# Last full block evicted and stored in halves, and a newly made order for the opening, in a tuned attention and gated feed-forward kernel

## The chip, the cores and the metric

The kernel runs on one core of one Trainium2 chip. The metric is the device time of one execution in microseconds (us); lower is better.

Names used throughout: TensorE (PE in the profile), VectorE (DVE), ScalarE (ACT), GpSimd (POOL), SyncE (SP, which here only issues transfers). PSUM is the memory that TensorE writes; it has banks. A **filler** is a matmul of a zero tile whose result nobody needs.

## The reference, cut to what matters

```python
B, N, m, C = (4, 12416, 32, 128)        # x: 4 x 12416 x 128; inducing: 32 x 128

def mab(q, kv):
    s = scale * (q @ kv.transpose(0, 2, 1))
    a = np.exp(s - s.max(-1, keepdims=True))
    a /= a.sum(-1, keepdims=True) + 1e-09
    return a @ kv
h = mab(I, x)            # 32 inducing rows look at all tokens of a batch
y = mab(x, h)            # all tokens look at those 32 rows
# then, for all 49664 tokens: out = (sigmoid(y @ w_gate) * (y @ w_val)) @ w_out,  d_ff = 1536
```

What matters: `h` of batch 0 needs *all* tokens of that batch. Until they have landed and been summed, nothing of the feed-forward part can start. That is the opening (some 28 us of 699). The later batches' sums run beside the feed-forward work of the batch before.

## The kernel before: the parts that the change touches

The program fixes the order of every engine by a list of names. These are the openings of the lists before (`xt` transposes of the input, `s1t` scores, `hv` sums of a tile into the accumulator, `hbase` two fp32 matmuls that fold the sums of tiles 0 to 4 together, `fill10.1` ten fillers, `s2t` the next scores, `fo` folds of the weights with `h`, `G` the first gate matmuls). A name like `hv5.8` is tile 5, slices from 8 on; the lists are cut after the opening.

```python
"PE": zero xt0.0 xt0.8 indT s1t0.0 xt1.0 hv0.0 s1t0.8 xt1.8 hv0.8 xt2.0 s1t1.0 s1t1.8 xt2.8 hv1.0 hv1.8 xt3.0 s1t2.0
      xt3.8 s1t3.0 s1t2.8 hv2.0 hv3.0 fill10.1 xt4.0 xt4.8 s1t3.8 hv2.8 s1t4.0 xt5.0 s1t4.8 xt5.8 hv3.8 hv4.0 hv4.8
      xt5.13 s1t5.8 s1t5.0 hbase s1t5.13 hv5.8 hv5.0 hv5.13 s2t0 fo0.1 s2t2 fo0.0 sb0.2 ... G0.0.3 ...
"POOL": cx0.0 cx1.0 cx2.0 cx3.0 cx4.0 cx5.0 cx5.8 wo wg.0 wv.0 wg.1 wv.1 ...      # cx: casts of x; wg, wv: of the weights
```

The accumulator `ACC` is one bank of PSUM, 512 fp32 columns. The sums, the values and the fillers have columns of their own in it:

```python
hsum, hval = ACC[:, 288:320], ACC[:, 256:288]

def h_base():            # sums of tiles 0 to 4: copy out, diagonal, two fp32 matmuls back in
    hev = dve(129, fin, "hev", lambda o: DVE.tensor_copy(out=hacc[0][:, 0 : P + 1], in_=ACC[:, 0 : P + 1]))
    sbc = dve(32, [hev], "hb0", lambda o: DVE.tensor_scalar_mul(out=ssb[0][:], in0=I4[:], scalar1=hacc[0][:, P : P + 1]))

    def em(o):
        PE.matmul(hval, lhsT=hacc[0][:, 0:P], rhs=I4[:], start=False, stop=False, skip_group_check=True)
        PE.matmul(hsum, lhsT=ones[:], rhs=ssb[0][:], start=False, stop=False, skip_group_check=True)
    fin[:] = [op("PE", 0.48, [hev, sbc], "hbase", em)]

def h_first():           # h of batch 0: VectorE reads the sums and the values
    r = dve(256, fin, "hr0", lambda o: DVE.reciprocal(out=hden[0][:], in_=hsum))
    hTd[0] = dve(32, [r], "hc0", lambda o: DVE.tensor_tensor(out=hT[0][:], in0=hval, in1=hden[0][:], op=ALU.mult))

def fill(o, n):
    for _ in range(n):
        PE.matmul(ACC[:, 320:512], lhsT=ident[:], rhs=zeros[:], start=False, stop=False, skip_group_check=True)
```

The end of a block of 512 tokens, which the change splits for the last full block:

```python
e = act(nt * P, ws + os.old, f"E{b}.{u}", lambda o: ACT.activation(
    out=os.t[:, 0:nt, :], in_=(psl(w) if alone else ACC)[:, 0 : nt * P], func=AF.Copy, scale=0.5), ...)
st = op("SP", 0.6, [e], f"st{b}.{u}", lambda o: SP.dma_start(ov[b][:, 4 * u : 4 * u + nt, :], os.t[:, 0:nt, :]), tail=8.0)
```

The softmax here doesn't subtract the row's maximum and nothing guards it: scores larger than these inputs give would overflow.

## Time and profile before

| | before |
|---|---|
| time, first three runs | 698.72 us median (698.71 to 699.49) |
| span of the profiled execution | 697.18 us |
| ScalarE busy in the middle 659.7 us | 658.7 us: the bound |
| last input cast on VectorE starts (**L**) | 20.16 us |
| reciprocal `hden` starts | 24.07 us, L + 3.91 |
| first gate tanh on ScalarE starts (**T**; the kernel takes the sigmoid by way of tanh) | 27.67 us, L + 7.51 |
| last big eviction starts (**E**) | 693.31 us, T + 665.64 |
| from E to the end | 3.87 us |

I use the marks L, T and E. The sum of the four stretches is the span: 20.16 + 7.51 + 665.64 + 3.87 = 697.18. The stretch up to L is set in the main by how the input lands and differs by 0.6 us from one execution to the next (19.82 to 20.39 in the profiles below), so it is taken out of each comparison by giving the reciprocal and T from L on.

These lines are from the timeline of the kernel before, in its opening. The columns are start, duration (us), engine, source line, operation, output and inputs with their shapes, and in brackets how long the engine had been idle and what it had waited for.

```profile
20.16 0.29 DVE L635 CAST x<-ua 128x256 f16<-128x256 f32 x1 [0.35 <-DMA ua<-in_x_dram]
21.47 1.03 POOL L635 CAST wg<-tga 128x1024 f16<-128x1024 f32 x1 [0.36 <-DMA tga<-in_moe_w_gate_dram]
21.95 0.58 DVE L635 TENSOR_SCALAR ssb<-I,hacc 128x32 f32<-128x32 f32 x1
24.07 0.36 DVE L635 RECIPROCAL hden<-acc 128x32 f32<-128x32 f32 x1 [1.21 <-PE acc L635]
25.49 0.39 PE L635 MATMUL g<-wv,hT 128*32 128x512 f16 x2
27.67 1.94 ACT L635 ACTIVATE tga<-g 128x1024 f16<-128x1024 f32 x2
```

The first line is L, the last is T. The bracket of the reciprocal: VectorE was idle for 1.21 us and waited for TensorE's writes to `acc`. The fold of the big weight tile (`g<-wv,hT`) starts 1.42 us after the reciprocal, and the first tanh 2.18 us after that fold.

### The profile page before, as it was taken

Reading aid. Unit: us, or ns where it says so; the run is one execution under the profiler, and the core shown is the slowest. Engines: PE = TensorE matmul, PEld = TensorE weight load, DVE = VectorE, ACT = ScalarE, POOL = GpSimd, SP = SyncE. Lnnn points to the kernel's source line nnn. Section 1 sums busy time; section 2 is a strip of 40 time slices with the busy share of each in tenths; the row PEclk is TensorE's granted clock in tenths of the full one; section 3 lists DMA queues with packets and bytes.
Section 4 is the critical chain, followed back from the end, with each engine's and each line's share of the span. In section 5 each row is a group of like instructions: output and inputs, shape, how many; then the busy total and the mean of one; then the engine's idle time right before and its main releaser. Section 6 shows DMA issues by size and latency. Waiting matters only on the chain.

```text
span 697.2 us, 20697 instructions
## 1 busy us (share of the span) xinstructions
PE 672.5 (96%) x8325; PEld 384.6 (55%) x8325; DVE 667.4 (96%) x1130; ACT 675.3 (97%) x867; POOL 435.8 (63%) x498
## 2 busy tenths in 40 slices
PE   7899999999999999999999999999999999999997
PEld 5545555555555555555555555555555555555555
DVE  4799999999999999999999999999999999999997
ACT  4899999999999999999999999999999999999995
POOL 4446756855739657766485575775674675667664
PEclk9999999999999999999999999999999999999999
DMA  9859796693655646746556559422333222242211
GB/s 352 190 127 184 162 176 157 134 184 85 146 129 135 133 109 156 149 117 140 107 123 155 122 106 140 141 71 87 88 113 109 56 85 99 63 131 89 83 48 50
DMA packets 121874, 87.72 MB, mean 126 GB/s; under 512 B 80913, under 2 KB 105009, under 8 KB 121777
## 3 DMA queue, kind: packets, MB, share of 16 engines
q1 hardware_dynamic: 117584, 76.44, 43.1%
q0 software_dynamic: 4144, 9.93, 9.2%
q8 instruction: 65, 1.06, 0.6%
q14 instruction: 33, 0.26, 0.1%
q10 hardware_dynamic: 48, 0.02, 0.0%
HBM read 39.99 MB, written 38.01 MB: 112 GB/s over the span
## 4 chain that ended last, share of the span: by engine, by line
PE 51%; ACT 26%; DVE 12%; issue 5%; DMA 3%; POOL 2%; SPq 0%; ACTq 0%; DVEq 0%; POOLq 0%
PE acc L635 26%; ACT tga L635 20%; PE v L635 17%; DVE ua L635 12%; PE g L635 8%; ACT vs L635 3%; ACT os L635 3%; DMA ua<-in_x_dram 2%; DMA xT<-in_x_dram 1%; DMA out_dram<-os 1%; POOL sm L635 0%; SPq L635 0%; POOL ua L635 0%; POOL pt L635 0%; ACT e L635 0%
## 5 line engine op out<-in xcount | busy, mean ns | idle before, releaser
L635 DVE SCALAR_TENSOR_TENSOR ua<-tga,v 128x512 f16<-128x512 f16 x1041 | 641.4, 682 | 10.6 <-PE v L635 3.0
L635 ACT ACTIVATE tga<-g 128x1024 f16<-128x1024 f32 x576 | 569.0, 1142 | 0.6 <-PE g L635 0.4
L635 PE MATMUL acc<-wo,ua 128*128 128x128 f16 x4608 | 358.8, 220 | 3.2 <-ACT os L635 0.2
L635 PEld LDWEIGHTS <-ua 128*128 128x128 f16 x4608 | 262.4, 98 | 169.2 <-issue 160.4
L635 PE MATMUL v<-a2r,hw 32*128 32x512 f16 x1200 | 322.3, 374 | 8.6 <-DVE ua L635 4.3
L635 POOL TENSOR_TENSOR pt<-tga,vs 128x512 f32<-128x512 f16 x111 | 129.1, 1163 | 171.4 <-ACT vs L635 73.6
L635 PE MATMUL g<-a2r,hw 32*128 32x512 f16 (+1 forms) x1200 | 225.7, 376 | 3.5 <-ACT tga L635 1.9
L635 PEld LDWEIGHTS <-hw 32*128 32x128 f16 x2400 | 88.7, 91 | 110.1 <-issue 44.0
L635 POOL TENSOR_TENSOR ua<-pt,vs 128x512 f16<-128x512 f32 x111 | 140.9, 1269 | 9.9 <-issue 1.2
L635 ACT COPY vs<-v 128x512 f32<-128x512 f32 x111 | 77.6, 701 | 0.2 <-PE v L635 0.2
L635 ACT ACTIVATE os<-acc 128x512 f32<-128x512 f32 (+1 forms) x99 | 68.9, 696 | 2.5 <-PE acc L635 2.4
L635 POOL TENSOR_TENSOR sm<-sm,minus 128x16 f32<-128x16 f32 (+1 forms) x21 | 63.9, 3043 | 1.6
L635 POOL TENSOR_TENSOR a2n<-e2t,sm 128x128 f16<-128x128 f16 x96 | 37.2, 482 | 1.3 <-DVE sm L635 0.4
L635 POOL DMA_DIRECT2D x<-in_x_dram x18 | 11.2, 621 | 41.5 <-ACT tga L635 40.1
L635 POOL TENSOR_TENSOR tree<-tree 128x64 f32<-128x64 f32 (+4 forms) x69 | 23.7, 343 | 5.4
L635 POOL TENSOR_TENSOR tree<-e2t 128x256 f32<-128x256 f16 (+1 forms) x23 | 15.8, 688 | 8.3 <-DMA e2t<-e 8.3
L635 ACT ACTIVATE e<-g 128x512 f16<-128x512 f32 (+1 forms) x23 | 17.0, 737 | 0.1
L635 DVE COPY xT<-g 128x1024 f16<-128x1024 f16 (+1 forms) x12 | 8.0, 666 | 8.5 <-PE g L635 8.5
L635 ACT ACTIVATE eT<-g 128x512 f16<-128x512 f32 (+1 forms) x18 | 13.0, 721 | 0.0
L635 PE MATMUL g<-ident,x 128*128 128x128 f16 x97 | 7.6, 220 | 2.7 <-ACT x L635 1.3
L635 PE MATMUL g<-xT,hT 128*32 128x512 f16 (+1 forms) x108 | 9.4, 363 | 0.0
L635 DVE SCALAR_TENSOR_TENSOR ut<-tgt,v 128x512 f16<-128x512 f16 (+1 forms) x16 | 8.7, 550 | 0.3 <-PE v L635 0.2
(83 smaller groups left out, 153.7 us busy)
## 6 DMA issues: line engine op xcount, KB each, us to landing
out_dram<-os SPq DMA_DIRECT2D x96, 256.0 KB, 2.5
a2r<-dr SPq DMA_DIRECT2D x23, 512.0 KB, 4.6
dr<-a2p SPq DMA_DIRECT2D x19, 512.0 KB, 3.5
x<-in_x_dram POOLq DMA_DIRECT2D x15, 512.0 KB, 5.6
xT<-in_x_dram SPq DMA_DIRECT2D x6, 512.0 KB, 7.4
dr<-a2p SPq DMA_DIRECT2D x4, 640.0 KB, 3.3
x<-in_x_dram POOLq DMA_DIRECT2D x3, 544.0 KB, 7.8
ua<-in_x_dram SPq DMA_DIRECT2D x3, 512.0 KB, 11.5
```

The source lines that it names most:

```text
L635: ins = fn(*a, **k)
```

## The change

Intent, as far as the edit shows it. (1) **Ending:** the last full block's 512-column eviction is done in two of 256 columns, each with a store of half the size, the first from SyncE's queue and the second from ScalarE's, so that the first half leaves earlier. (2) **Opening:** the model from which the order lists were made gets the measured landing of the input (410 instead of 421 thousand bytes per us, and 1.25 us more for the second half of tile 4), the measured length of `ssb` and of a transfer's issue on GpSimd. The lists of the opening are then made anew. The constants are only used to make the order; the code that runs changes by the order alone.

The diff, cut to its core (ScalarE's list of the opening, cut here, is reordered in the same way; the rest of the lists only renumbers the fillers):

```diff
 "PE":
-        zero xt0.0 xt0.8 indT s1t0.0 xt1.0 hv0.0 s1t0.8 xt1.8 hv0.8 xt2.0 s1t1.0 s1t1.8 xt2.8 hv1.0 hv1.8 xt3.0 s1t2.0
-        xt3.8 s1t3.0 s1t2.8 hv2.0 hv3.0 fill10.1 xt4.0 xt4.8 s1t3.8 hv2.8 s1t4.0 xt5.0 s1t4.8 xt5.8 hv3.8 hv4.0 hv4.8
-        xt5.13 s1t5.8 s1t5.0 hbase s1t5.13 hv5.8 hv5.0 hv5.13 s2t0 fo0.1 s2t2 fo0.0 sb0.2 ...
+        zero xt0.0 xt0.8 indT s1t0.8 xt1.8 xt1.0 s1t0.0 xt2.0 s1t1.0 hv0.8 hv0.0 s1t1.8 xt2.8 s1t2.0 hv1.0 xt3.0 xt3.8
+        hv2.0 s1t2.8 s1t3.0 xt4.0 hv2.8 s1t3.8 hv3.0 hv1.8 s1t4.0 fill8.1 xt4.8 hv3.8 xt5.0 xt5.8 s1t4.8 hv4.0 xt5.13
+        s1t5.0 s1t5.8 hv4.8 s1t5.13 hv5.0 hv5.8 hv5.13 hbase fill10.2 s2t0 fo0.1 s2t2 fo0.0 sb0.2 ...
 "ACT": ... (casts and exponentials of the opening reordered)
+        T3.24.0 E3.22 E3.24 E3.23 Eh3.23 sth3.23
 "DVE":
-        ind16 xc0.0 indTc xc0.8 xc1.0 xc1.8 ... xc4.8 cx5.13 xc5.0 hev hb0 xc5.13 hr0 hc0 ...
+        xc0.0 ind16 xc0.8 indTc xc1.8 xc1.0 ... xc4.8 cx5.13 xc5.0 xc5.13 hev hb0 hr0 hc0 ...
 "POOL":
-        ... cx5.8 wo wg.0 wv.0 wg.1 wv.1 ld1.0 ...
+        ... cx5.8 wo wg.0 wg.1 wv.1 wv.0 ld1.0 ...
 def load(dst, src, nbytes, name):
-        landed[0] += nbytes / 421e3
+        landed[0] += nbytes / 410e3 + (1.25 if name == "lx4.8" else 0)
...
-        e = act(nt * P, ws + os.old, f"E{b}.{u}", ...)
+        for k in range(2 if (b, u) == (B - 1, NB - 1) else 1):
+            lo, hi = (2 * k, 2 * k + 2) if (b, u) == (B - 1, NB - 1) else (0, nt)
+            x = "h" * k
+            e = act((hi - lo) * P, ws + os.old, f"E{x}{b}.{u}", ...  os.t[:, lo:hi, :] <- [:, lo * P : hi * P] ...)
+            q, n = (ACT, "ACT") if k else (SP, "SP")
+            st = op(n, 0.6, [e], f"st{x}{b}.{u}", lambda o, lo=lo, hi=hi, q=q: q.dma_start(
+                ov[b][:, 4 * u + lo : 4 * u + hi, :], os.t[:, lo:hi, :]), tail=8.0)
...
-        st = op("SP", 0.6, [e], f"st{b}.{u}", lambda o: SP.dma_start(ov[b][:, 4 * u : 4 * u + nt, :], os.t[:, 0:nt, :]), ...)
```

On VectorE, `hev` and `hb0` (the copy `hacc` and the diagonal `ssb`) move behind the copy of the last transposes (`xc5.13`); on TensorE, `hbase` moves behind all the sums of tile 5; and `fill10.2`, ten fillers, stands between `hbase` and the rest.

## The prediction

> **What bounds the kernel now.** I read the busy table of three stretches first, then the groups, then the chain of waits of the opening, then the timeline around its ends. The table has, after the stretch and its length, the busy time of TensorE, its weight loads, VectorE, ScalarE and GpSimd, then clock, DMA share and GB/s.
>
> ```profile
> 0.00:27.60 27.60, 22.26 (x390) 15.23 (x394) 13.55 (x39) 14.82 (x30) 13.03 (x27) 1.00 0.91 305
> 27.60:687.30 659.70, 644.35 (x7867) 365.18 (x7866) 648.41 (x1083) 658.72 (x835) 420.63 (x470) 1.00 0.52 119
> 687.30:697.20 9.90, 5.93 (x76) 4.22 (x74) 5.46 (x10) 1.76 (x4) 2.12 (x2) 0.90 0.17 61
> ```
>
> In the middle ScalarE is busy 658.72 of 659.70 us: it is the bound, with 0.98 us of idle. The group line agrees:
>
> ```profile
> L635 ACT ACTIVATE tga<-g 128x1024 f16<-128x1024 f32 x576 | 569.0, 1142 | 0.6 <-PE g L635 0.4
> ```
>
> So the time is: start of the first gate tanh (27.67 us) + a rigid middle + an ending. The change's order lists differ only before the first gate and after the last, so a shift of the first tanh moves the end by the same amount. The opening ends with this chain (start, duration, what; us):
>
> ```profile
> 8.43 11.04 DMA ua<-in_x_dram
> ...
> 20.92 0.60 PE acc L635 x24
> 21.52 0.02 issue
> 21.54 0.30 DVE hacc L635
> ...
> 21.95 0.60 DVE ssb L635
> 22.55 0.04 issue
> 22.59 0.41 PE acc L635 x2
> 23.00 0.18 PE v L635 x4
> 23.19 0.86 PE acc L635 x34
> 24.05 0.02 issue
> 24.07 0.37 DVE hden L635
> ...
> 24.46 0.20 DVE hT L635
> ```
>
> The reader is to see that the input lands until about 20.1, and that four more microseconds pass until the reciprocal (hden) starts at 24.07: the sums of tiles 0 to 4 (acc x24), their copy (hacc), the diagonal (ssb), two fp32 matmuls (acc x2, called hbase here), then the sums of tile 5 (acc x34). From hT to the first tanh it is 27.67 - 24.46 = 3.21 us. The two cheap-looking things that matter below are the ten filler matmuls, which write the unused columns of acc, and the ending:
>
> ```profile
> 16.24 1.00 PE L635 MATMUL acc<-zeros,ident 128*128 128x192 f16 x10
> 17.07 0.50 PE L635 MATMUL g<-ident,x 128*128 128x128 f16 x6
> 693.31 0.60 ACT L635 ACTIVATE os<-acc 128x512 f32<-128x512 f32 x1 [2.42 <-PE acc L635]
> out_dram<-os SPq DMA_DIRECT2D x96, 256.0 KB, 2.5
> out_dram<-os SPq DMA_DIRECT2D x4, 64.0 KB, 1.9
> ```
>
> Ten fillers hold TensorE 17.07 - 16.24 = 0.83 us. After the last eviction (ends 693.91) a 256 KB store and the closing waits take until 697.2.
>
> **What the Trainium skill says.** (1) "PSUM — Partial Sum Buffer", section "PSUM bank collisions raise a hardware error": two engines may not touch one bank in one quadrant at once, whatever the columns, and the compiler puts a wait between them. The trace before has no filler just ahead of a read of acc, so it does not show the cost; the built program of the changed kernel does show such a wait (below). (2) "DMA: Bandwidth & Descriptors", "Anatomy of one DMA": about 2.0 us fixed plus bytes/436e9. That page's fit is for GpSimd's queue; it gives 2.6 us for 256 KB and 2.15 for 64 KB, and the trace has 2.5 and 1.9 on SyncE's queue: near enough. (3) Same page, "Issuing engines are not separate DMA queues": a second issuing engine saves only issue time; the issue is 0.33 us here. (4) "ScalarE: Activation LUTs", "What ACT_TABLE_LOAD costs": 186 ns + 0.833 ns a column, and neighbours overlap by 93 ns. For 512 columns 0.61; the trace has 0.60.
>
> **The change part by part: the ending.** One 512-column eviction becomes two of 256: estimated from the skill's formula 0.40 each, the second ending 0.40 + 0.40 - 0.09 = 0.71 after the start instead of 0.60. So the second half's store is issued about 0.1 later than the whole one was. Each store is 128 KB: between the trace's 1.9 (64 KB) and 2.5 (256 KB), interpolated by bytes 2.1, so 0.4 shorter; the first half's bytes are mostly out before the second's begin. Sum: +0.1 - 0.4 = **-0.3 us**.
>
> **The opening.** The order of the loads is not changed, so I expect the same landings. I walk the new order with the durations of the trace before. The transpose of the last slices waits, old and new, for the copy of tile 5's first half, which stands behind the last cast on VectorE and ends at 20.38 + 0.68 = 21.06. Old: transpose at 21.42, because 24 sum matmuls stood in front; new: 21.14. ScalarE's copy of the middle slices starts at about 20.6 instead of 21.02. So the new order is **ahead by 0.3 to 0.4 us** here. Then:
> - Exponentials of tile 4's half: ScalarE 21.2 to 21.6; their sums 21.8 to 22.1; copy hacc 22.1 to 22.4; ssb 22.5 to 23.1 (0.29 and 0.58 as before). Old: hacc at 21.54. The new order puts hacc **0.6 later**.
> - The program's waits show that tile 5's sums now wait for hacc (same bank): 22.5. The 34 matmuls take 0.86: to about 23.3.
> - hbase now comes last, after them: two fp32 matmuls, about 0.3 each (their weight loads are 0.30 for two): to about 24.0. In the old order these lay in the wait for the last copy and cost almost nothing at the end.
> - Then ten fillers, new here: 0.83, to about 24.8. In the built program the reciprocal's wait counts up to **the last of these fillers**; before it counted up to the last sum of tile 5. With the old 0.2 us from the last issue to the reciprocal (23.86 to 24.07): the reciprocal at about **25.0 instead of 24.07, +0.9 us**.
> - Weights: GpSimd casts now the two small tiles before the big value tile. The small ones land at about 23.4 and 24.1 (issue at 13.55 and 14.84 plus 9.8 and 9.3), so the big one ends at 24.1 + 0.6 + 1.0 = 25.75; its fold stood at 25.49. With the shift above the fold would be at 26.4: hidden.
> From hT on, the order is the old one: the first tanh at 27.67 + 0.9 = 28.6.
>
> Sum: 698.72 + 0.9 - 0.3 = **699.3 us**.
>
> **Rivals.** (a) The wait on the fillers costs nothing, or they run while the reciprocal's inputs are still pending: then the reciprocal is at about 24.15 to 24.2, +0.1. Now the weight cast binds: fold at 25.8 instead of 25.49, +0.3 at the first tanh. Total 698.72 + 0.3 - 0.3 = 698.7. Against it: the wait is in the program. (b) The plan of the change holds: last tile 0.3 earlier, carried through, and the ending's 0.3: 698.1. For it: the PE stalls between 15.6 and 21 are real. Against it: hbase and the copy moved behind the last sums, and the landing itself does not move. (c) The second store is slower than thought (both share the same 16 engines, and ScalarE's queue was last used at 0.72 us): ending 0, total 699.6. (d) The early part falls behind: the first projection of scores moves from 7.99 to about 8.5, and the casts of ScalarE up to 12.7 are delayed by up to 0.7. Landings are 1.25 us apart and each tile needs 0.7 of VectorE and about 1.1 of TensorE, so I expect it caught up by tile 4, which lands 1.2 late (17.37).
>
> **Range and chances.** The opening's sum has an error of about 0.4 (six estimated steps of 0.1 to 0.2), the ending's 0.15, and the three runs before spread over 0.8. Rival (a) is inside the range, (b) outside. 8 in 10: 698.6 to 700.0. 2% is 14 us, some ten times anything here: within 2% 0.98.
>
> **What would show it.** In the changed profile: reciprocal hden at 24.8 to 25.3, directly after ten fillers; hacc at 22.1; first transpose of the last four slices near 21.15; first gate tanh at 28.3 to 28.8; two 256-column evictions of 0.37 to 0.40; from the end of the last sum (693.29 before) to the end of the span 3.6 instead of 3.9 us; middle ScalarE idle still about 1 us. I would be wrong if hden starts before the fillers end, if the first tanh is not later, or if the middle takes the shift up.

## The result, and the profile after

The changed kernel is correct. It took 699.43 us median of 4 runs (699.15 to 699.53); the kernel before, in the same rounds, 699.06 (698.71 to 699.49). The ratio of the two is 1.0004 with a 95% interval of 0.9987 to 1.0022: the same. (A ratio is the mean time of one kernel's fast runs over that of the other's of the same rounds, so it is not quite the ratio of the medians.)

The busy table of three stretches of the changed kernel, with the columns as in the prediction:

```profile
0.00:28.30 28.30, 22.88 (x394) 16.59 (x394) 12.87 (x39) 14.60 (x30) 13.10 (x27) 0.94 0.88 296
28.30:687.90 659.60, 644.16 (x7866) 365.49 (x7864) 648.04 (x1083) 658.57 (x835) 420.34 (x470) 1.00 0.53 119
687.90:697.80 9.90, 6.12 (x79) 4.33 (x76) 5.65 (x10) 2.03 (x5) 2.34 (x2) 0.95 0.18 61
```

The middle is as before: ScalarE busy for 658.57 of 659.60 us. The first tanh comes 0.86 us later (28.53 against 27.67). The opening's chain of waits (start, duration, what):

```profile
21.26 0.38 PE g L636 x4
...
22.24 0.30 DVE hacc L636
...
22.59 2.31 PE acc L636 x48
...
24.93 0.37 DVE hden L636
```

Where the chain before had two fp32 matmuls, four small ones and 34 sums ahead of the reciprocal, it now has one piece of 2.31 us, 48 instructions long, all of TensorE into `acc`. The timeline splits that piece:

```profile
22.65 0.24 DVE L636 TENSOR_SCALAR ssb<-I,hacc 128x32 f32<-128x32 f32 x1
23.45 0.39 PE L636 MATMUL acc<-I,hacc 128*128 128x32 f32 x2
23.90 0.99 PE L636 MATMUL acc<-zeros,ident 128*128 128x192 f16 x10
24.42 1.60 POOL L636 CAST wv<-tga 128x512 f16<-128x512 f32 x2 [0.25 <-DMA tga<-in_moe_w_val_dram]
24.93 0.36 DVE L636 RECIPROCAL hden<-acc 128x32 f32<-128x32 f32 x1 [2.04 <-PE acc L636]
26.27 0.39 PE L636 MATMUL g<-wv,hT 128*32 128x512 f16 x2
28.53 1.02 ACT L636 ACTIVATE tga<-g 128x1024 f16<-128x1024 f32 x1
```

Sums of tile 5 from 22.59, `hbase` from 23.45, ten fillers from 23.90; the reciprocal starts only at 24.93, after 2.04 us of idle VectorE, and the first tanh at 28.53. At the end, the timeline's eviction and the list of transfers:

```profile
694.11 0.66 ACT L636 ACTIVATE os<-acc 128x256 f32<-128x256 f32 x2 [2.41 <-PE acc L636]
out_dram<-os SPq DMA_DIRECT2D x1, 128.0 KB, 1.7
out_dram<-os ACTq DMA_DIRECT2D x1, 128.0 KB, 1.8
```

In the columns of the list: the queue, how many, the size, and the us from issue to landing. The whole store of 256 KB in the kernel before took 2.0 us in the same place.

The span went from 697.18 to 697.76, +0.58 us. By the four stretches: up to L +0.15 (L differs as much between executions of one kernel), from L to T **+0.71**, middle -0.06, from E to the end **-0.22** (3.87 to 3.65).

### The profile page after: what moved, and what is told of

Same layout as the page of the kernel before. It is cut to its first block, busy times and chain, and to the rows that moved or that the text cites. A ratio compares the mean times of both kernels' runs of the same rounds, so it can differ in the third digit from the quotient of the medians.

```text
span 697.8 us, 20718 instructions
## 1 busy us (share of the span) xinstructions
PE 673.2 (96%) x8333; PEld 386.4 (55%) x8333; DVE 666.6 (96%) x1130; ACT 675.2 (97%) x868; POOL 435.8 (62%) x498
## 4 chain that ended last, share of the span: by engine, by line
PE 51%; ACT 26%; DVE 13%; issue 5%; DMA 3%; POOL 1%; SPq 0%; ACTq 0%; DVEq 0%
PE acc L636 26%; ACT tga L636 19%; PE v L636 17%; DVE ua L636 12%; PE g L636 8%; ACT os L636 3%; ACT vs L636 3%; DMA ua<-in_x_dram 2%; DMA xT<-in_x_dram 1%; DMA out_dram<-os 1%; SPq L636 0%; POOL sm L636 0%; ACT tgt L636 0%; ACT e L636 0%; POOL a2n L636 0%
## 5 line engine op out<-in xcount | busy, mean ns | idle before, releaser
L636 ACT ACTIVATE os<-acc 128x512 f32<-128x512 f32 (+2 forms) x100 | 69.1, 692 | 2.5 <-PE acc L636 2.4
```

What stands on the lines that cost most here:

```text
L636: ins = fn(*a, **k)
```

## The experiments

Twelve kernels ran besides the two, in three groups, each group on one chip with its own runs of the kernel before. All gave correct results. The kernel before took 699.43 us (698.55 to 705.37) in the first group (tail_only, no_fill, fill20, fill_v), 698.74 (698.29 to 702.02) in the second (best1, early_h, old_fill, wt_old) and 698.84 (698.44 to 702.11) in the third; compare times within a group only. The interval of every ratio to the kernel before includes 1, so the readings below rest on the marks of each profile, one profile a kernel (us):

| kernel | what it is | L | reciprocal - L | T - L | E to end | time: median (range), runs |
|---|---|---|---|---|---|---|
| before | | 20.16 | 3.91 | 7.51 | 3.87 | 699.06 (698.71-699.49), 4 |
| after | | 20.31 | 4.62 | 8.22 | 3.65 | 699.43 (699.15-699.53), 4 |
| tail_only | before + new ending | 20.20 | 3.92 | 7.51 | 3.65 | 699.02 (698.56-699.42), 6 |
| pro_only | after with old ending | 20.02 | 4.62 | 8.22 | 3.87 | 699.66 (699.18-700.17), 4 |
| tail_1q | tail_only, one queue | 20.03 | 3.92 | 7.52 | 3.76 | 700.13 (698.38-701.66), 4 |
| no_fill | after, fillers out | 20.11 | 3.80 | 8.73 (half clock) | 3.65 | 699.61 (698.51-706.52), 6 |
| fill20 | after, 20 fillers | 20.31 | 5.44 | 9.03 | 3.66 | 700.45 (700.23-700.59), 4 |
| fill_v | after, fillers in another bank | 20.06 | 3.79 | 7.81 | 3.64 | 698.60 (698.59-698.82), 4 |
| old_fill | before + fillers, same bank | 19.95 | 4.74 | 8.35 | 3.87 | 699.32 (699.30-699.35), 4 |
| old_vfill | before + fillers, other bank | 19.86 | 3.92 | 7.60 | 3.87 | 698.65 (698.43-698.88), 5 |
| wt_old | after, old order of weights | 20.39 | 5.01 | 8.61 | 3.64 | 699.57 (699.33-699.75), 4 |
| best1 | fill_v, old order of weights | 19.82 | 3.79 | 7.39 | 3.65 | 698.46 (698.29-698.80), 6 |
| early_h | best1, `hbase`'s inputs sooner | 20.04 | 3.66 | 7.69 | 3.66 | 698.68 (698.37-699.05), 4 |
| best_nofill | best1, fillers out | 20.06 | 3.79 | 7.39 | 3.65 | 699.04 (698.43-699.62), 5 |

In every ordinary profile the stretch from T to E is between 665.3 and 665.7 us, whatever the opening did. The stretches add up; what is gained or lost at T or after E stays. Some executions took over 700 us for another reason, the clock, which has its own part below. They are within 1.5% of the fastest and count as fast in the ratios of this document.

**The theory:** the reciprocal waits for the ten fillers, because they write the same PSUM bank as the sums that it reads, and this wait is nearly all of the opening's loss. **Rivals:** the loss is TensorE's time as such, wherever the fillers write; or the new order itself (`hbase` last); or the weights' new order.

### What the fillers cost: fill20, no_fill, fill_v, old_fill, old_vfill

fill20 doubles the suspected cost.

```diff
- ... hv5.13 hbase fill10.2 s2t0 ...
+ ... hv5.13 hbase fill20.2 s2t0 ...
```

> The changed kernel with twenty fillers instead of ten. If hden waits for the last filler: hden at 24.93 + 0.83 = 25.76, first gate tanh at 29.36, time +0.83 us over the changed kernel. If the fillers are hidden: nothing moves.

Its timeline:

```profile
23.89 1.81 PE L636 MATMUL acc<-zeros,ident 128*128 128x192 f16 x20
25.75 0.36 DVE L636 RECIPROCAL hden<-acc 128x32 f32<-128x32 f32 x1 [2.87 <-PE acc L636]
```

The last cast starts at 20.31 in both kernels, the fillers within 0.01 us of each other, and the reciprocal is 0.82 us later, T 0.81. The four times are all above all of the changed kernel's (measured in another group). Ten fillers more cost 0.8 us.

no_fill takes them out.

```diff
- ... hv5.13 hbase fill10.2 s2t0 ...
+ ... hv5.13 hbase s2t0 ...
```

> The changed kernel without the ten fillers ahead of the reciprocal. My theory: hden then waits for the last fp32 matmul only and starts at about 24.1 instead of 24.93; but the big value-weight cast on GpSimd (ends 26.02 in the changed profile) then holds its fold at about 26.08 instead of 26.27, so the first gate tanh comes at about 28.3 instead of 28.53: only 0.2 us of the 0.83 come back. Rival (the fillers' wait is the whole cost): first tanh at about 27.7 and 0.8 us under the changed kernel. Second rival (fillers cost nothing): hden stays at 24.9.

From its timeline:

```profile
23.91 0.36 DVE L636 RECIPROCAL hden<-acc 128x32 f32<-128x32 f32 x1 [1.21 <-PE acc L636]
```

With L at 20.11, the reciprocal comes 3.80 after L instead of 4.62: 0.82 us gained, and 0.11 us *sooner* than in the kernel before. So the rival "the new order itself" falls: without its fillers the new order is not slower up to the reciprocal. Its profile fell into a stretch of half clock from the fold on, so its T tells nothing.

fill_v keeps the ten fillers in their place and lets them write a tile of another bank.

```diff
+ def em(o, n=n):          # "vfill10.2", a tile of its own from the pool of v tiles
+     for _ in range(n):
+         PE.matmul(psl(o)[:, 320:512], lhsT=ident[:], rhs=zeros[:], start=True, stop=True)
- ... hv5.13 hbase fill10.2 s2t0 ...
+ ... hv5.13 hbase vfill10.2 s2t0 ...
```

> The ten fillers kept, but written to another PSUM bank (a v tile) instead of the unused columns of acc. If the cost is the wait for the shared bank: hden at about 24.1 although TensorE is busy with fillers until about 24.75; scores after hT then start at 24.75 to 24.8 and the value weights bind as without fillers (first tanh about 28.3). If the cost is TensorE's time for the fillers: hden stays at 24.9.

Its timeline:

```profile
23.64 0.99 PE L636 MATMUL v<-zeros,ident 128*128 128x192 f16 x10
23.85 0.36 DVE L636 RECIPROCAL hden<-acc 128x32 f32<-128x32 f32 x1 [1.21 <-PE acc L636]
24.18 1.60 POOL L636 CAST wv<-tga 128x512 f16<-128x512 f32 x2 [0.25 <-DMA tga<-in_moe_w_val_dram]
25.83 0.39 PE L636 MATMUL g<-wv,hT 128*32 128x512 f16 x2
```

The fillers take the same 0.99 us on TensorE, and the reciprocal starts 0.21 us after the *first* of them: 3.79 after L. TensorE's own time is hidden; the wait went with the bank. It is a wait that the program holds: as built, the reciprocal waits until TensorE's count reaches 341 in the changed kernel (the last filler), 351 with twenty, and 331 (the second matmul of `hbase`) here and in no_fill. But T came only 0.41 us sooner (L + 7.81 against 8.22): the cast of the big value tile, now last in GpSimd's order, ends at 24.18 + 1.60 = 25.78, and the fold starts 0.05 us after it. Half of the gain turned into a new wait. The time was 698.60, all four runs below all of the changed kernel's, again in another group.

old_fill and old_vfill add the same ten fillers to the *old* order, after its last sums: first in the accumulator's bank, then in another.

```diff
- ... hv5.8 hv5.0 hv5.13 s2t0 ...
+ ... hv5.8 hv5.0 hv5.13 fill10.2 s2t0 ...      # old_fill
+ ... hv5.8 hv5.0 hv5.13 vfill10.2 s2t0 ...     # old_vfill
```

> The kernel before with ten fillers into acc put directly after its last sums. If the wait on the shared bank is the cost in any order: hden at 24.07 + 0.83 = 24.9, first gate tanh at 28.5, time 0.8 us over the kernel before. If the fillers cost only in the new order: nothing moves.

> The kernel before with ten fillers behind the last tile's sums, as in old_fill, but written to another bank of PSUM (a v tile). Theory (what the fillers cost is the wait of the reciprocal on a shared bank): the reciprocal starts 3.9 us after the last input tile's cast begins, as in the kernel before, and not 4.7 as in old_fill; first gate tanh 7.5 to 7.6 after that cast; time as undisturbed runs of the kernel before, 698.4 to 698.8. Rival (the fillers delay the path by TensorE's own time): reciprocal 4.7 after the cast. Second theory (fillers keep TensorE's clock up): none of the executions over 700 us, against some 16 in 100 of kernels without them. Rival: as many as in the kernel before of the same rounds.

From the timelines, old_fill first and old_vfill second:

```profile
23.67 0.99 PE L635 MATMUL acc<-zeros,ident 128*128 128x192 f16 x10
24.69 0.36 DVE L635 RECIPROCAL hden<-acc 128x32 f32<-128x32 f32 x1 [2.04 <-PE acc L635]
```

```profile
23.59 0.98 PE L635 MATMUL v<-zeros,ident 128*128 128x192 f16 x10
23.78 0.36 DVE L635 RECIPROCAL hden<-acc 128x32 f32<-128x32 f32 x1 [1.21 <-PE acc L635]
```

In the accumulator's bank: L + 4.74, the kernel before plus 0.83. In another: L + 3.92, the kernel before (T is L + 7.60, 0.09 later than there). So the cost is the same in both orders, is proportional to the number of fillers, and goes with the bank. The theory is shown, and its rivals for the reciprocal fall. One thing these runs can't separate: the accumulator is one PSUM tile of the program and fills exactly one bank, so they don't tell whether the wait was put in for the tile or for the bank.

### What the weights' order does: wt_old, best1, early_h

wt_old is the changed kernel with GpSimd's casts of the weights in the old order; best1 is the same edit on fill_v. The two differ by the fillers' bank alone.

```diff
- ... cx5.8 wo wg.0 wg.1 wv.1 wv.0 ...
+ ... cx5.8 wo wg.0 wv.0 wg.1 wv.1 ...
```

> The changed kernel with only the weight casts put back into the order of the kernel before. My theory: behind the filler wait they are hidden; first gate tanh at 28.5 as in the changed kernel, time the same within 0.1 us. Rival (the weights' order is the cost): first tanh back to 27.7 to 28.1.

> The changed kernel with the fillers in another PSUM bank and the four weight casts on GpSimd in the order of the kernel before. My theory: hden stays 3.8 us after the last cast's start, as in the run with the fillers in a v tile; the big value cast now ends before 24 instead of 25.78, so its fold comes at about 25.4 instead of 25.83 and the first gate tanh at about 27.55 instead of 27.87; time about 0.3 us under that run (698.3) and 0.4 under the undisturbed runs of the kernel before. Rival (the fold was not what held the first tanh): 27.87 again.

wt_old did not come out as hoped for a clean reading: already the last cast on VectorE took 0.69 us in its profile instead of 0.29, and the copy `hacc` came 2.32 after L instead of 1.93. From that copy to the reciprocal it took 2.69 us, exactly as in the changed kernel, and to T 6.29, also the same. So with the fillers' wait in place the weights' order is worth nothing; the slow start in that profile is explained in part. Its trace has GpSimd's casts of two middle tiles some 0.46 us later than in the changed kernel, both waiting for their input (12.79 and 15.37 us against 12.33 and 14.90). TensorE, equally late, ran the eight fillers of `fill8.1` at 18.48 (18.04 in the changed kernel), so that the next transposes began at 19.13, although ScalarE had finished their input at 18.28; and the last cast on VectorE followed the work before it without a wait for its input. Why that cast took 0.69 us is not shown.

best1's timeline:

```profile
23.61 0.36 DVE L636 RECIPROCAL hden<-acc 128x32 f32<-128x32 f32 x1 [1.21 <-PE acc L636]
23.98 0.61 POOL L636 CAST wv<-tga 128x512 f16<-128x512 f32 x1
```

The reciprocal is where fill_v has it (L + 3.79), but now the last weight cast is done at 24.59, and T comes 7.39 after L, 0.42 sooner than in fill_v. best1 took 698.29 to 698.80 in six runs, wt_old 699.33 to 699.75 in four, on one chip: no overlap, a difference of the medians of 1.11 us for the bank alone. (0.4 us of it is wt_old's odd opening, if its other runs had it too.) best1 is also 0.34 us below the kernel before by its parts (0.12 by T, 0.22 by the ending). Its time against the kernel before is 0.9989 (0.9975 to 1.0004): that sign, but not resolved (without the kernel before's two executions over 700 us the means are 698.51 and 698.72).

early_h asks whether the new order has more to give: the sums of tile 4's second half and their exponentials move ahead of other work, so that `hbase`'s inputs come sooner.

```diff
- PE:  ... s1t5.0 s1t5.8 hv4.8 s1t5.13 ...        ACT: ... xc5.8 xs1t4.8 xs1t5.0 ...
+ PE:  ... s1t5.0 hv4.8 s1t5.8 s1t5.13 ...        ACT: ... xs1t4.8 xc5.8 xs1t5.0 ...
```

> As the run before it, and with the sums of tile 4's last half moved ahead (their exponential before ScalarE's copy, their matmuls before the projection of the middle slices), so that hacc can start at about 21.6 instead of 22.0. My theory: hden comes about 0.3 to 0.4 earlier (23.5), but the fold of the small value tile waits for its cast (24.85) in TensorE's order, so the first gate tanh gains at most 0.1 us. Rival (the chain through hden still sets the start): first tanh 0.3 to 0.4 earlier.

The reciprocal gained 0.13 us, but T came 0.30 later than in best1 (L + 7.69): in this run the small value tile landed late, and its fold at 25.16 had waited 0.35 us for GpSimd's cast. The size for the reciprocal was missed (0.3 to 0.4 expected); that the small value tile's cast would hold the fold came true. In this profile the landing of the weights was the next limit; one profile doesn't show where that limit lies in general.

### The ending: tail_only, pro_only, tail_1q

tail_only is the kernel before with the new ending; pro_only is the changed kernel with the old one; tail_1q is tail_only with both half stores on SyncE's queue.

```diff
 # tail_only: the loop over k of the change, on the kernel before; pro_only: the change without it
 # tail_1q:
-            q, n = (ACT, "ACT") if k else (SP, "SP")
+            q, n = SP, "SP"
```

> The kernel before with the halved ending alone. My theory: the ending is worth about -0.2 us (the changed profile: from the start of the last eviction to the end of the span 3.69 us against 3.87), the opening's reciprocal hden stays at 24.07 and the first gate tanh at 27.67; so 0.2 us under the kernel before. Rival (the second store gains nothing, the 0.18 was chance between two profiles): 3.87 again and the same time.

> The changed kernel with the old ending: new order of the opening alone. Theory (parts add up): reciprocal 4.6 us after the last cast, first tanh 8.2 after it, from the last eviction's start to the end 3.87; so 0.2 us more than the changed kernel, 699.2 to 699.8. Rival (the ending's halves gain nothing on the chip): to the end 3.7 and the changed kernel's own time.

> The kernel before with its last full block evicted and stored in halves, but both stores from SyncE's queue. Theory (halving the eviction gives the gain, and the second queue saves only issue time): from the start of the first half eviction to the end of the span 3.65 to 3.80 us, against 3.66 with two queues and 3.87 with one whole store. Rival (the second queue is what gains): 3.85 us or more. Time 698.4 to 699.4, not to be told from the kernel before.

The stretch from E to the end falls into three values. It is 3.87 us with one eviction and one store, in all four kernels that have it (before, pro_only, old_fill, old_vfill). It is 3.64 to 3.66 with halves on two queues, in all nine (no_fill's slow profile too has 3.65). With halves on one queue it is 3.76, and there the timeline shows the two issues one behind the other on SyncE:

```profile
693.26 0.81 SPq L635 DMA_DIRECT2D out_dram<-os  x2
```

So the halving is worth 0.11 and the second queue another 0.11. The second issue starts 0.83 us after E on SyncE's queue and 0.69 on ScalarE's, and the stores themselves take much the same (1.77 and 1.81 us): what the second queue saves is the wait for the first issue. In the times nothing of it can be seen: tail_only's ratio to the kernel before is 0.9981 with an interval of 0.9953 to 1.0009, and that ratio leans on three executions of the kernel before over 700 us; without them the means are 698.99 and 699.04. pro_only confirms that the parts add: L + 4.62, L + 8.22 as in the changed kernel, and 3.87 at the end.

### The slow executions: no_fill, best_nofill

In this part "slow" means a lower granted clock of TensorE; by the rule of 1.5% all these runs still count as fast. The kernel before has executions above 700 us now and then (702.0, 705.4 and 702.1 among 11 in the first group). The mean granted clock of TensorE is lower in just these: 0.989 to 0.994, where that kernel's others have 0.997 or more. no_fill's profile happened to catch one (706.52 us, clock 0.983). Two stretches of it, columns as in the busy tables:

```profile
34.00:38.00 4.00, 4.00 (x30) 2.14 (x27) 2.94 (x6) 2.81 (x3) 0.21 (x1) 0.50 0.19 37
50.00:54.00 4.00, 4.00 (x42) 2.08 (x41) 4.00 (x8) 3.68 (x6) 0.65 (x2) 1.00 0.87 191
```

From 25.58 us on, about where the big fold starts, for 23.89 us in the trace's record of the clock (seven windows of 3.41 us), TensorE ran at half clock while it was busy nearly all the time (3.66 to 4.00 of every 4 us from 26 to 50); VectorE and ScalarE starved behind it (2.94 and 2.81 of 4 us). That is a second purpose that the new fillers may have: to keep TensorE busy while it waits for `h`. best_nofill tests it on best1.

```diff
- ... hv5.13 hbase vfill10.2 s2t0 ...
+ ... hv5.13 hbase s2t0 ...
```

> best1 without its ten fillers. Theory (fillers in another bank cost nothing and are there for the clock): in an undisturbed profile the reciprocal 3.8 us after the last cast and first tanh 7.4 after it, as in best1; undisturbed runs 698.4 to 698.8; one execution or more over 700 us. Rival (the fillers have nothing to do with the slow executions): none over 700 us beyond what the kernel before shows in the same rounds. If the fillers themselves cost time although in another bank: reciprocal 0.1 us earlier than in best1 or more.

Its reciprocal and T are those of best1 (L + 3.79, L + 7.39), so in these two profiles fillers in another bank cost nothing. But none of its five executions was slow, against my expectation of one or more. Counting all runs by their clock (0.994 or less): 9 of 56 executions of kernels without fillers between the last sums and the next scores were slow (6 of 35 of the kernel before, 1 of 6 of no_fill, 2 of 4 of tail_1q, none of 6 of tail_only and 5 of best_nofill), and 0 of 39 of kernels with them. (no_fill has two more at 0.995 with 699.6 us, which are not counted.) If the nine had fallen at random on the 95 executions, all would miss the 39 in 0.6 of 100 cases. That speaks for the theory. But I made the count after two groups had suggested it; in the third group alone it is 3 of 18 against 0 of 9, which chance gives in 28 of 100. And the count mixes fillers with the order: 30 of the 39 executions with fillers are of the new order, 45 of the 56 without are of the old. Within the old order it is 8 of 45 against 0 of 9 (chance: 21 of 100), within the new 1 of 11 against 0 of 30 (27 of 100). So that the order, and not the fillers, keeps the clock up is a rival that no run here excludes. What makes the half clock begin in one execution and not in the next is not shown: TensorE was busy for 3.09 of the 4 us from 22 to 26 in no_fill's slow execution, and for 3.16 in the changed kernel's. **This stays open.**

## Why the prediction was right

The prediction said 699.3 us (698.6 to 700.0) and "same"; the kernel took 699.43. Its steps, one by one:

- **Rigid middle, the first tanh carries to the end: right.** T to E was 665.58, before 665.64.
- **Start of the last transposes (21.14) and `hacc` at 22.1, +0.6: right in size.** 21.26 and 22.24; taken from L, `hacc` was at + 1.93 where the prediction had 1.94.
- **Tile 5's sums wait for `hacc`, then 0.86 us: right.** 22.59 to 23.45.
- **`hbase` costs its whole length behind the sums: right in mechanism, mis-sized.** The step "two fp32 matmuls, about 0.3 each" and its rounding up to 24.0 gave 0.7 us; it took 0.45 (23.45 to 23.90).
- **The reciprocal's wait counts to the last filler, 0.83 us: right**, by three pairs (after against no_fill 0.82, fill20 against after 0.82, old_fill against before 0.83). The mechanism that it names, the shared bank, is shown by fill_v and old_vfill, which keep the fillers and lose the wait.
- **What the order alone does:** rival (a) gave +0.1 for the reciprocal; it was -0.12 (no_fill, fill_v, best1 at L + 3.79 to 3.80 against 3.91). The difference is the `hbase` term above. An order that puts `hbase` last is even a little quicker, and one reason shows in the lines of before: `ssb`, then on the chain, started at 21.95 while GpSimd cast a weight tile (21.47 to 22.50), and took 0.58 us to 22.53. In the changed kernel the cast ended as `ssb` began at 22.65; it took 0.24 and lay beside the sums anyway. The Trainium skill, "SBUF — State Buffer", section "Who interferes with whom", has it that a VectorE copy or tensor_scalar in a two-port mode and a GpSimd instruction hold a shared port against each other for a whole instruction. The traces agree as far as they go. In the six profiles in which `ssb` began some 0.55 us before the end of a cast (before, tail_only, tail_1q, old_fill, old_vfill, wt_old) it took 0.58 to 0.61 us and ended 0.03 to 0.04 us after the cast did. It took 0.24 in the others, in early_h too, where the cast still ran for its first 0.14 us. That the port is the cause was not tested.
- **Weights hidden: right, with little to spare.** The last cast ended at 26.02, 0.27 later than worked out, and the fold began at 26.27. Rival (a)'s second half, that the weights would bind if the fillers' wait went away, came true in fill_v: T 0.3 above L + 7.51.
- **First tanh +0.9: 0.86 in the two profiles**, of which 0.15 is the later landing; the change's own part is 0.71.
- **Ending -0.3: right in sign, mis-sized.** It was -0.22. The failed term is the store: the prediction took 2.5 us for 256 KB from a group's median over the whole run and put 2.1 for 128 KB. At the end, with nothing else on the queues, they took 2.04 and 1.80: -0.24 in place of -0.4. The second issue's start was +0.07 (0.62 and 0.69 us after E), near the +0.1 worked out. The rest, -0.05, is in the closing waits after the landing (1.21 and 1.16 us), which the prediction left as they were.

Two of the errors went opposite ways (0.2 too much lost in the opening, 0.1 too much gained at the end), the landing added 0.15, and the time of the kernel before from which it started (698.72, the middle of three runs) was 0.34 below its median with the fourth run (699.06). The total was good to 0.13 us partly by luck; the parts are what was right. Rival (b), the plan of the change, is refuted as it was run; rival (c) did not happen. Of (d) the delay came (the first projection of scores at 8.49 us, as worked out), and it was caught up as the prediction expected. What nobody foresaw: TensorE's clock was halved for one window from 10.82 to 14.23 us. Six of the nine profiles with the new order have such a window there, beginning between 9.3 and 10.9, and none of the five with the old order. From 6 to 10 us TensorE was busy for 1.93 to 2.60 of 4 us in the new order and for 2.98 to 3.40 in the old. It did no harm at L: fill20, which has no such window, has L at 20.31 like the changed kernel.

## What to carry to other kernels

Instructions that only keep an engine busy were not free in this kernel when they wrote the PSUM tile that another engine was about to read: the program made the reader wait for the last of them, unused columns or not. Give fillers a bank of their own; here that was worth 0.8 us at the reciprocal, and only 0.4 at the first tanh until the next wait, a weight cast that had been moved back because it was hidden, was moved up again. When a change moves an instruction "out of the way", look for what its hiding rests on: here that slack was 0.25 us, and it came from the very wait that one would want to remove.

## What the Trainium skill lacked or had wrong

- "PSUM — Partial Sum Buffer", "PSUM bank collisions raise a hardware error": it says that a dependency is added, not what it costs. Here: 0.082 us for each 192-column filler that stands ahead of the reader in the bank (0.82 us for ten, 1.64 for twenty, both against no_fill), and nothing for ten in another bank.
- "DMA: Bandwidth & Descriptors", "Anatomy of one DMA": the page gives this fit for GpSimd's queue alone: 2.0 us plus bytes over 436e9, which is 2.15, 2.3 and 2.6 us for 64, 128 and 256 KB. It has none for the other queues. On SyncE's and ScalarE's queues at the quiet end of this kernel it was 1.5, 1.7 to 1.8 and 2.0 us.
- "TensorE: Matmul & The Clock Gate", "What's actually happening": full rate is said to follow after at least one busy window of some 3.4 us. In no_fill's profile the half rate lasted 23.89 us, seven such windows, with TensorE shown as busy 4.00 of 4.00 us from 26 to 46. The page doesn't say what counts as busy, and so doesn't explain this.
